# Two more chunks inverted in blocks of 32 steps, and the preparation dealt anew, in a chunked RWKV-7 and squared-ReLU kernel

## The chip, the cores and the metric

The kernel runs on one core of a Trainium2 chip, in float32. The metric is the device time of one execution in microseconds. A program of one core has one time; the times below are the median of a few runs, and one further execution was taken with the hardware profiler.

## What is computed

For each of 4 batches and 8 heads a state of 40 x 40 runs over 768 steps, and each step is read out before it changes the state. The result, 3072 tokens of 320 numbers, goes through a feed-forward layer with a squared ReLU.

```python
state = np.zeros((B, H, D, D))                     # B, H, S, D = 4, 8, 768, 40
for t in range(S):
    kt, vt, rt = k[:, :, t], v[:, :, t], r[:, :, t]
    wt, at, bt = w[:, :, t], a[:, :, t], b[:, :, t]
    y[:, :, t] = np.einsum('bhd,bhde->bhe', rt, state)
    Sa = np.einsum('bhde,bhe->bhd', state, at)
    state_decay = state * wt[:, :, None, :] - np.einsum('bhd,bhe->bhde', Sa, bt)
    state = state_decay + np.einsum('bhd,bhe->bhde', vt, kt)
...
x = y.transpose(0, 2, 1, 3).reshape(3072, 320)
h = np.maximum(x @ w_in, 0.0)                      # 320 x 2048
out = h * h @ w_out                                # 2048 x 320
```

## The kernel before

**Chunks and slots.** The 768 steps of a batch are cut into 6 chunks of 128 steps. There are 24 chunks, numbered so that the batch runs fastest: chunks 0 to 3 are the first chunks of the four batches, 4 to 7 the second ones. The main loop has one slot a chunk. A slot runs the chunk's `chain`: it brings in what the state gives, solves for the removed part x with the matrices T and N, updates the state, and makes the chunk's tokens (line 684, the last step of the chain). Within the same slot, in an order that is written out by hand (`woven` for slots 0 to 3, `sorted_slot` from slot 4 on), lie the preparation of the next chunk (`turn_rv`, `turn_k`, `make_a`, `make_rv`, `scale_kb`, `decay_state`), the feed-forward layer of chunks that are done (`second`), and the early part of chunks further ahead.

**Early parts.** `early` needs only w, a and b of a chunk. It takes cumulated products of w (lines 352 and 353), their reciprocals (357, 358), products with a and b (364, 365) and the triangular matrix `N` of the chunk, 128 x 128 for each head (line 372 ff.). It stores the decays (`kept_e`), the upper right block of N (`kept_n`), and what has to be inverted. The table `ahead` says which early parts a slot makes. A slot with two makes the first (`one`) at the places of the single one and the second (`two`) at later places; the stores of a second part leave after the slot's chain, together with the token moves and the loads of the next slot.

**The inversion on GpSimd.** Each head's chunk has two triangular blocks of 64 x 64 whose inverses the chain needs. GpSimd finds them by substitution (`solving`): for every step one product (line 448) and one subtraction (line 450), on 128 partitions, over all chunks of a *unit*. A unit is a run of chunks that are inverted together: chunk 0; 1; 2 and 3; 4 and 5; 6 and 7; 8 and 9; 10 to 13; 14 to 17; 18 to 21; 22 and 23 (units 0 to 9). `take` (line 420) loads a unit's blocks from `kept_q` or `kept_d` in device memory into `half_n`, and line 453 stores the inverses from `half_t` to `kept_t`. GpSimd's instructions run in their order, so a unit starts when the one before it is stored and when the blocks of all its chunks have landed. The main loop emits a unit when the early parts of all its chunks are done.

**Fine and coarse units.** The number `FINE` divides the units. Units below it are *fine*: their blocks are halved once more to 32 x 32 (31 steps instead of 63), stored in `kept_q`, with the block that joins two halves in `kept_m`. What the joining takes is done later by other engines in `inverses`: a transposition of the loaded inverses on VectorE (line 482), two activations (line 484), two times 16 products of 32 x 32 on TensorE, and copies (lines 494 and 501). A coarse unit's inverse comes from `kept_t` straight into T (line 464). Before, units 0 to 3 are fine.

**A unit in two pieces.** Unit 4, `AHEAD`, is emitted in two pieces: 33 steps after its load; then, when unit 5 can be emitted, the first 2048 words a row of unit 5 are loaded, the rest of unit 4 runs, and the rest of unit 5 is loaded.

**Loads.** All loads and stores but GpSimd's go through SyncE's queue, in the order in which they are written. `loads(j)` loads chunk j's decays (`dec`), k and b; r and v come one at a time through `fetch_next`. At the end of slot 3 the loads for slot 4's preparation of chunk 5 are issued as dec, k, b and then v. `later` holds a store back for a step or two; what stands behind it in that list waits with it.

Of the kernel before, what the change touches and what calls it, by code (L numbers as in the profile page):

```python
# [17 lines left out]
def kernel(  # L18
# [29 lines left out]
    HC = C // 2  # L48
# [11 lines left out]
    at = 0  # L60
# [31 lines left out]
    def new(name, shape, bufs):  # L92
        return work.tile(shape, FP32, tag=name, name=name, bufs=bufs)
# [7 lines left out]
    def tick():  # L101
        for entry in line:
            entry[0] -= 1
        while line and line[0][0] <= 0:
            line.pop(0)[1]()
# [10 lines left out]
    class Ring:  # L116
# [6 lines left out]
        def next(self):  # L123
            self.at = (self.at + 1) % len(self.tiles)
            return self.tiles[self.at]
# [10 lines left out]
    order = [(bb, c) for c in range(NCH) for bb in range(B)]  # L136
    loaded, early_loaded = {}, {}

    def fetch(ring, src, i):
        bb, c = order[i]  # L140
        t_ = rings[ring].next()
        nc.sync.dma_start(out=t_[:, :, :D], in_=src[bb, :, c * C:(c + 1) * C, :].rearrange("h t d -> t h d"))
        return t_
# [137 lines left out]
    def as_they_are():  # L281
# [4 lines left out]
        for f in range(NF):  # L286
# [8 lines left out]
    Q = HC // 2  # L295
# [2 lines left out]
    sizes = [1, 1] + [2] * 4 + [4] * ((len(order) - 12) // 4) + [2]  # L298
    units = [(sum(sizes[:u]), n) for u, n in enumerate(sizes)]

    FINE = 4
    SMALL = units[FINE][0]
    kept_q = dram.tile([SMALL, H, 2, 2, Q, Q], FP32, tag="q", name="kept_q")
    kept_m = [dram.tile([2, Q, H, Q], FP32, tag=f"m{i}", name=f"kept_m{i}") for i in range(SMALL)]
# [3 lines left out]

    classes = lambda u: 128 // (units[u][1] * (4 if u < FINE else 2) * H)
    kept_t = [dram.tile([classes(u), nb, H, 2, 2, Q // classes(u), Q] if u < FINE else [classes(u), nb, H, 2, HC // classes(u), HC], FP32,  # L310
                        tag=f"t{u}", name=f"kept_t{u}") for u, (_, nb) in enumerate(units)]
# [93 lines left out]

    part_of = lambda u: given[:, u % 3 * Q * Q:(u % 3 + 1) * Q * Q] if u < FINE else given


    EARLIER = Q * HC

    def take(u, queues, words=slice(None)):
        first, nb = units[u]
        if u < FINE:
            kept = kept_q[first:first + nb].rearrange("b h f k s t -> (b h f k) (s t)")
        else:
            kept = kept_d[u].rearrange("b h f w -> (b h f) w")
        cols = classes(u)
        rows = 128 // cols
        for col in range(cols):
            queues[col % len(queues)].dma_start(out=part_of(u)[col * rows:(col + 1) * rows, words], in_=kept[:, words])  # L420

    def solve(u, between={}):
        run(solving(u, between))

    def solving(u, between={}, stop=None):

        first, nb = units[u]
        fine = u < FINE
        size = Q if fine else HC
        cols = classes(u)  # L430
        rows = 128 // cols
        part = part_of(u)
        words = size // cols * size
        at = u * Q * Q // 2 if fine else 0
        ts = solved[:, at:at + words]
        nc.gpsimd.memset(ts, 0.0)
        for col in range(cols):
            nc.gpsimd.memset(ts[col * rows:(col + 1) * rows, col::size + cols], -1.0)
        t3 = ts.rearrange("p (j t) -> p j t", t=size)
        for s in range(size - 1):  # L440
            if s in between:
                between[s]()
            if s == stop:
                yield
            n, m_ = s // cols + 1, size - 1 - s
            at = s * size + s + 1 if s < Q else Q * HC + (s - Q) * (Q + 1) + 1
            p_ = new("half_p", [128, 528], 1)[:, :n * m_].rearrange("p (j t) -> p j t", j=n)
            nc.gpsimd.tensor_tensor(p_, part[:, at:at + m_].unsqueeze(1).to_broadcast([128, n, m_]),  # L448
                                    t3[:, :n, s:s + 1].to_broadcast([128, n, m_]), Alu.mult)
            nc.gpsimd.tensor_tensor(t3[:, :n, s + 1:], t3[:, :n, s + 1:], p_, Alu.subtract)  # L450
        to = kept_t[u]
        to = to.rearrange("n b h f k j t -> (n b h f k) (j t)") if fine else to.rearrange("n b h f j t -> (n b h f) (j t)")
        nc.gpsimd.dma_start(out=to, in_=ts)
# [331 lines left out]
    def run(gen):  # L785
        for _ in gen:
            tick()
# [28 lines left out]
    own = [nc.gpsimd]  # L816

    def flush():
        while line:
            tick()  # L820
# [58 lines left out]


    TOTAL = 12
    ahead = {0: (4, 5), 1: (6, 7), 2: (8, 9), 3: (10,), 4: (11,), 5: (12, 13)}
    ahead.update({i: (i + 8,) for i in range(6, 9)})
    ahead[9] = (17, 18)
    ahead.update({i: (i + 9,) for i in range(10, len(order) - 9)})

    pieces_in = {0: (4, TOTAL), 1: (6, TOTAL), 2: (6, TOTAL), 3: (7, TOTAL)}
    done = set(range(B))
    unit = unit_of[B]

    AHEAD, under_way = (FINE,), []

    def woven(i, g, ch):
        jobs = [(ch, 11, 0, TOTAL)]
        made = ahead.get(i, ())
        for j, m_ in enumerate(made):
            jobs.append((prepare(m_), 5, j * 5, TOTAL - 5 * (len(made) - 1 - j)))
        if i:
            ready[i + 1] = {}
            load(i + 1, ready[i + 1])  # L900
        jobs.append((rest(i + 1, ready[i + 1]), 9, 2, TOTAL))
        m_, end = pieces_in[i]
        jobs.append((some(rounded, 2 * m_), 2 * m_, 0, end))
        weave(*jobs)

    def fetch_next(i, *names):
        if i < len(order):
            loaded.setdefault(i, {}).update({nm: fetch(nm, {"k": k, "b": b, "r": r, "v": v}[nm], i) for nm in names})

    def loads(j):  # L910
        if j < len(order):
            n = ready.setdefault(j, {})
            n["dec"] = kept_here[j % 2]
            nc.sync.dma_start(out=n["dec"][:USED], in_=kept_e[j])
            fetch_next(j, "k", "b")
# [65 lines left out]
    for i in range(len(order)):  # L981
        tc.no_sync_barrier()
        g = ready.pop(i)
        ch = first_slot if i == 0 else g["chain"]
        done.update(ahead.get(i, ()))
        if i < B:
            woven(i, g, ch)
            n = ready[i + 1]
            n["chain"] = chain(i + 1, n)
            next(n["chain"])  # L990
            if i == B - 1:
                loads(i + 2)
                fetch_next(i + 2, "v")
        else:
            sorted_slot(i, g, ch)
        while unit < len(units) and all(m_ in done for m_ in range(len(order)) if unit_of[m_] == unit):
            flush()
            if under_way:

                take(unit, own, slice(0, EARLIER))  # L1000
                run(under_way.pop())
                take(unit, own, slice(EARLIER, Q * (HC + Q)))
            else:
                take(unit, own)
            if unit in AHEAD:
                under_way.append(solving(unit, stop=Q + 1))
                next(under_way[0])
            else:
                solve(unit)
            unit += 1  # L1010
    flush()
    second.rest()
# [30 lines left out]
```

## Time and profile before

| | |
|---|---|
| median of 3 runs | 1040.03 us (1037.89 to 1045.76) |
| the profiled execution | 1038.23 us |
| its span from first to last instruction | 1036.5 us |
| TensorE busy in the span | 907.5 us (88%) |
| its weight loads | 756.3 us (73%) |
| GpSimd busy | 672.7 us (65%) |
| VectorE busy | 484.4 us (47%) |
| ScalarE busy | 285.2 us (28%) |

The page gives busy time by engine and, below that, the span in 40 slices of 25.9 us, with a digit for the tenths in which the engine was busy (9 is 90% or more). PE is TensorE, PEld its weight load, DVE VectorE, ACT ScalarE, POOL GpSimd, SPq the queue of SyncE, which issues transfers. PEclk is the clock that TensorE was granted, in tenths of full speed, and DMA the mean busy share of the 16 DMA engines.

A row of a timeline has the start in us, the duration in us, engine, line and operation, what is written and read, how many such instructions stand together, and in brackets the idle time of the engine before them and what ended it. A row of the busy time by stage has the stretch, its length, the busy time of TensorE, its weight loads, VectorE, ScalarE and GpSimd with the number of instructions, then clock, DMA share and GB/s.

### The profile page before, as it was taken

How to read it: one execution, taken by the hardware profiler on the slowest of the kernel's cores; microseconds unless marked ns; L12 is line 12 of the kernel's file. 1: busy time of each engine (PE TensorE's matmuls, PEld its weight loads, DVE VectorE, ACT ScalarE, POOL GpSimd, SP SyncE). 2: the span in 40 equal slices, each digit the busy share in tenths (PEclk: the TensorE clock that was granted, in tenths of full speed). 3: DMA queues.
4: the chain of work that ended last, by engine and by line, in shares of the span. 5: the costliest groups of instructions: out<-in, count | busy, mean ns of one | idle time of the engine just before them, and what ended most of it. 6: DMA issues, size and time to landing. Idle time of an engine off the chain costs nothing.

```text
span 1036.5 us, 19696 instructions
## 1 busy us (share of the span) xinstructions
PE 907.5 (88%) x7728; PEld 756.3 (73%) x7728; DVE 484.4 (47%) x864; ACT 285.2 (28%) x663; POOL 672.7 (65%) x1128
## 2 busy tenths in 40 slices
PE   6465664684799999999599999999999999999998
PEld 5454563674688888888388888788888888887776
DVE  5556675765457346656066544624433233321111
ACT  3132423143323322332123222322222322232111
POOL 4788462898798359999599994999967981000000
PEclk9666565656799999999699999999999999999999
DMA  8977979795433894663785776553346434130000
GB/s 105 160 140 146 177 157 172 164 178 120 78 84 80 157 175 87 117 90 65 178 145 88 103 114 158 106 82 59 69 109 104 67 56 95 31 65 8 14 13 13
DMA packets 261376, 106.92 MB, mean 103 GB/s; under 512 B 244100, under 2 KB 250372, under 8 KB 259620
## 3 DMA queue, kind: packets, MB, share of 16 engines
q1 hardware_dynamic: 256756, 86.65, 47.5%
q0 software_dynamic: 3440, 18.88, 7.8%
q8 instruction: 61, 1.00, 0.4%
q10 hardware_dynamic: 1088, 0.13, 0.1%
q14 instruction: 31, 0.25, 0.1%
HBM read 72.47 MB, written 31.19 MB: 100 GB/s over the span
## 4 chain that ended last, share of the span: by engine, by line
PE 57%; POOL 14%; DMA 11%; DVE 5%; ACT 4%; issue 4%; SPq 4%; ACTq 0%; POOLq 0%; DVEq 0%
PE ps_f L87 30%; PE ps_c L87 12%; PE ps_w L87 9%; POOL half_t L450 7%; POOL half_p L448 6%; PE ps_w L316 3%; SPq L108 2%; DMA in_v<-in_v_dram 2%; DMA blocks<-kept_t 2%; DMA dec<-kept_e 1%; DMA half_n<-kept_d 1%; DMA kept_t<-half_t 1%; PE ps_c L651 1%; PE ps_c L560 1%; DMA in_k<-in_k_dram 1%
## 5 line engine op out<-in xcount | busy, mean ns | idle before, releaser
L448 POOL TENSOR_TENSOR half_p<-half_n,half_t 128x70 f32<-128x70 f32 (+52 forms) x502 | 298.3, 594 | 94.2 <-DMA half_n<-kept_d 43.5
L450 POOL TENSOR_TENSOR half_t<-half_t,half_p 128x70 f32<-128x70 f32 (+52 forms) x502 | 324.9, 647 | 39.3
L87 PE MATMUL ps_f<-w_out,hid 128*128 128x320 f32 x768 | 219.3, 435 | 0.0
L87 PEld LDWEIGHTS ps_f<-w_out,hid 128*128 128x128 f32 x768 | 141.3, 190 | 54.4 <-issue 3.4
L87 PE MATMUL ps_f<-tokens,w_in 128*128 128x256 f32 x672 | 158.7, 390 | 0.0
L87 PEld LDWEIGHTS ps_f<-tokens,w_in 128*128 128x128 f32 x672 | 127.5, 195 | 18.4 <-issue 1.0
L743 DVE TENSOR_TENSOR hid<-hid 128x512 f32<-128x512 f32 x96 | 88.8, 961 | 49.7 <-ACT hid L736 49.7
L736 ACT ACTIVATE hid<-ps_f 128x512 f32<-128x512 f32 x84 | 50.2, 598 | 97.9 <-PE ps_f L87 97.3
L684 DVE TENSOR_TENSOR tokens<-ps_c,dec 128x512 f32<-128x512 f32 x24 | 16.6, 691 | 92.2 <-PE ps_c L87 92.2
L532 DVE TENSOR_TENSOR f<-end,dec 128x4 f32<-128x4 f32 x20 | 7.1, 355 | 112.1 <-DMA dec<-kept_e 112.1
L352 DVE TENSOR_TENSOR_SCAN decay<-ps_w,ones 128x64 f32<-128x64 f32 x88 | 23.7, 270 | 65.7 <-PE ps_w L316 65.7
L87 PEld LDWEIGHTS ps_c<-xr,T 64*64 64x64 f32 x768 | 29.8, 148 | 32.9 <-issue 27.8
L615 ACT COPY xnT<-ps_c 64x512 f32<-64x512 f32 x24 | 13.9, 579 | 143.8 <-PE ps_c L87 143.7
L87 PE MATMUL ps_w<-decay,bT 40*128 40x128 f32 x352 | 31.9, 327 | 23.2 <-DVE decay L365 21.3
L372 ACT COPY N<-ps_w 128x512 f32<-128x512 f32 x24 | 14.1, 586 | 135.3 <-PE ps_w L87 106.6
L332 DVE TENSOR_TENSOR RV<-ps_w,upper 128x512 f32<-128x512 f32 x48 | 30.9, 686 | 42.4 <-PE ps_w L87 41.9
L87 PE MATMUL ps_f<-tokens,w_third 64*128 64x256 f32 x336 | 47.0, 391 | 3.9 <-DVE w_out L266 3.9
L510 DVE TENSOR_TENSOR kvT<-ps_w,dec 128x512 f32<-128x512 f32 x24 | 16.3, 681 | 70.7 <-ACT minus_x L638 33.6
L87 PE MATMUL ps_c<-xr,T 64*64 64x40 f32 x768 | 35.7, 242 | 15.2 <-DMA tokens<-tokens 12.8
L87 PEld LDWEIGHTS ps_w<-decay,bT 40*128 40x128 f32 x352 | 29.2, 231 | 26.7 <-issue 14.7
L332 DVE TENSOR_TENSOR RX<-ps_w,upper 128x512 f32<-128x512 f32 x48 | 30.9, 686 | 26.9 <-PE ps_w L87 26.8
L357 DVE RECIPROCAL decay<-decay 128x256 f32<-128x256 f32 x22 | 38.2, 1737 | 0.0
(136 smaller groups left out, 1484.0 us busy)
## 6 DMA issues: line engine op xcount, KB each, us to landing
kept_e<-decay SPq DMA_DIRECT2D x22, 633.8 KB
dec<-kept_e SPq DMA_DIRECT2D x22, 633.8 KB
hid<-in_moe_w_out_dram SPq DMA_DIRECT2D x16, 320.0 KB
half_n<-kept_d POOLq DMA_DIRECT2D x6, 768.0 KB, 11.9
in_w<-in_w_dram SPq DMA_DIRECT2D x24, 160.0 KB
in_ab<-in_b_dram SPq DMA_DIRECT2D x24, 160.0 KB
in_ab<-in_a_dram SPq DMA_DIRECT2D x24, 160.0 KB
in_k<-in_k_dram SPq DMA_DIRECT2D x24, 160.0 KB
```

Source lines behind the costliest of these rows:

```text
L87: nc.tensor.matmul(o, l_, r_, start=start, stop=True, skip_group_check=True)
L108: later(lambda: queue.dma_start(out=out_, in_=in_), steps)
L316: nc.tensor.transpose(p_[:, q * 128:(q + 1) * 128], pair(x_, q), ident)
L332: nc.vector.tensor_tensor(t_, p_, over4(upper), Alu.mult)
L352: nc.vector.tensor_tensor_scan(up[:, q, MID + 1:C + 1], wT[:, q, MID:], ones, 1.0, Alu.mult, Alu.mult)
L357: nc.vector.reciprocal(down[:, :, MID + 1:C + 1], up[:, :, MID + 1:C + 1])
L448: nc.gpsimd.tensor_tensor(p_, part[:, at:at + m_].unsqueeze(1).to_broadcast([128, n, m_]), t3[:, :n, s:s + 1].to_broadcast([128, n, m_]), ...
L450: nc.gpsimd.tensor_tensor(t3[:, :n, s + 1:], t3[:, :n, s + 1:], p_, Alu.subtract)
L510: nc.vector.tensor_tensor(kT, kT_, down[:, :, 1:C + 1], Alu.mult)
L684: nc.vector.tensor_tensor(t_, y_, g["up"][:, :, :C], Alu.mult)
L736: nc.scalar.activation(h_, p_.rearrange("p f t -> p (f t)"), Act.Relu)
L743: nc.vector.tensor_tensor(h_, h_, h_, Alu.mult)
```

## The change

Unit 4 (chunks 6 and 7) becomes fine. Its place in `half_t` is that of unit 0. Every unit is now emitted whole. In `ahead`, slot 4 makes chunks 11 and 12 and slot 5 makes 13 and 14, and from slot 6 to slot 14 slot i makes chunk i + 9; before, slot 4 made 11, slot 5 made 12 and 13, slots 6 to 8 made chunk i + 8, and slot 9 made 17 and 18. At the end of slot 3, v of chunk 5 is loaded ahead of dec, k and b.

```diff
-    FINE = 4
+    FINE = 5
...
-        at = u * Q * Q // 2 if fine else 0
+        at = u % 4 * Q * Q // 2 if fine else 0
...
-    ahead = {0: (4, 5), 1: (6, 7), 2: (8, 9), 3: (10,), 4: (11,), 5: (12, 13)}
-    ahead.update({i: (i + 8,) for i in range(6, 9)})
-    ahead[9] = (17, 18)
-    ahead.update({i: (i + 9,) for i in range(10, len(order) - 9)})
+    ahead = {0: (4, 5), 1: (6, 7), 2: (8, 9), 3: (10,), 4: (11, 12), 5: (13, 14)}
+    ahead.update({i: (i + 9,) for i in range(6, len(order) - 9)})
...
-    AHEAD, under_way = (FINE,), []
...
             if i == B - 1:
+                fetch_next(i + 2, "v")
                 loads(i + 2)
-                fetch_next(i + 2, "v")
...
-            if under_way:
-
-                take(unit, own, slice(0, EARLIER))
-                run(under_way.pop())
-                take(unit, own, slice(EARLIER, Q * (HC + Q)))
-            else:
-                take(unit, own)
-            if unit in AHEAD:
-                under_way.append(solving(unit, stop=Q + 1))
-                next(under_way[0])
-            else:
-                solve(unit)
+            take(unit, own)
+            solve(unit)
             unit += 1
```

## The prediction

> **What bounds the kernel now.** I read the forty slices first, then busy time by stage, the gaps on TensorE, GpSimd's own list and SyncE's queue. Slot i is the stretch that ends when line 684 writes chunk i's tokens: slots 1 to 5 end at 147.34, 201.93, 240.15, 304.21 and 341.63 us, slots 8 to 10 at 446.01, 482.61 and 538.25.
>
> ```profile
> PE   6465664684799999999599999999999999999998
> ...
> POOL 4788462898798359999599994999967981000000
> PEclk9666565656799999999699999999999999999999
> DMA  8977979795433894663785776553346434130000
> ```
>
> From the twelfth slice on TensorE is full, but for one slice. Before that, in slots 1 to 4, it is half busy while the DMA engines are near full. The same by slot (busy us of TensorE, weight loads, VectorE, ScalarE, GpSimd; clock; DMA):
>
> ```profile
> 377.29:411.65 34.36, 34.36 (x317) 29.28 (x314) 18.47 (x32) 10.10 (x24) 31.61 (x36) 1.00 0.64 106
> 446.01:482.61 36.60, 36.28 (x328) 30.99 (x326) 25.70 (x43) 10.12 (x24) 33.93 (x35) 1.00 0.58 91
> 482.61:538.25 55.64, 41.56 (x332) 34.50 (x330) 18.15 (x31) 11.70 (x28) 41.56 (x65) 0.82 0.67 138
> 641.35:678.05 36.70, 35.18 (x316) 29.77 (x314) 17.71 (x31) 10.11 (x24) 29.18 (x41) 1.00 0.62 116
> ```
>
> A slot with one early part is 34.36 us, all TensorE. Slot 10 is 55.64. TensorE's list says where it stood, and the chain of waits what ended it: GpSimd's store of unit 6 and the load of T.
>
> ```profile
> 509.01 1.08 PE L87 MATMUL ps_c<-xr,T 64*64 64x40 f32 x16 [12.82 <-DMA tokens<-tokens]
> ```
> ```profile
> 494.61 5.30 DMA kept_t<-half_t
> 500.61 8.31 DMA T<-kept_t
> ```
>
> GpSimd needed 134.9 us from the load of unit 6 (359.75) to its store (494.61). It began late not for want of time: it had stored unit 5 at 345.34 and waited for the blocks of chunk 13.
>
> ```profile
> 345.34 0.60 POOL L453 DMA_DIRECT2D kept_t<-half_t  x1 [0.30 <-POOL half_t L450]
> 359.75 1.03 POOL L420 DMA_DIRECT2D half_n<-kept_d  x2 [13.81 <-DMA kept_d<-N]
> ```
>
> SyncE's queue shows why. Slot 5's first early part (chunk 12) leaves at 334.71, its second (13) only at 351.64, behind the token moves and chunk 7's loads:
>
> ```profile
> 334.71 1.82 SPq L108 DMA_DIRECT2D kept_d<-N  x4
> ...
> 351.64 6.25 SPq L108 DMA_DIRECT2D kept_d<-N  x4
> ```
>
> Three further gaps on TensorE stand in slots 2 and 4, all on loads:
>
> ```profile
> 170.52 1.11 PE L316 MATMUL ps_w<-ident,in_k 128*128 128x128 f32 x4 [5.93 <-DMA in_k<-in_k_dram]
> ...
> 182.40 1.09 PE L316 MATMUL ps_w<-ident,in_w 128*128 128x128 f32 x4 [7.89 <-DMA in_w<-in_w_dram]
> ...
> 260.47 1.09 PE L316 MATMUL ps_w<-ident,in_v 128*128 128x128 f32 x4 [12.84 <-DMA in_v<-in_v_dram]
> ```
>
> **What the Trainium skill says.** "DMA: Bandwidth & Descriptors", section "Issuing engines are not separate DMA queues": transfers started by SyncE and GpSimd run on the same 16 engines and interleave. The trace agrees: from 161 to 183 us SyncE's queue takes 73.9% and GpSimd's 35.6% of the engines, more than 100% together, while slot 2's loads are late. "TensorE: Matmul & The Clock Gate", Part 1: after a few us of idling TensorE runs at half clock. Agreed: 0.50 granted between 500 and 513 us, and 16 rows of xr,T take 1.08 us against 0.66 us elsewhere, so a gap costs a little more than itself. "GPSIMD Engine Reference", section 8: GpSimd shares its SBUF interfaces with VectorE. Agreed: a line-450 subtraction of 273 elements took 1.13 us once and 0.71 us another time; units 4 and 5, the same 126 operations, took 76.7 and 80.9 us.
>
> **The change part by part**, against the profiled execution's 1038.23 us (span 1036.5 plus 1.7 around it), which lies 1.8 below the median and within the runs.
>
> *Unit 4 in blocks of 32.* Its compute becomes unit 3's, 27.1 us (121.25 to 148.38), for 76.7. Taken from 161.5, it ends near 201. Unit 5 then waits for chunk 9, loads near 211 in one piece, starts near 228 and ends near 309. GpSimd's 50 us are not on the path as such: unit 6 waits for chunk 13 in either case. Worth 0; if that cover were gone, unit 6 would be late by whatever unit 5 lacks of about 32 us of spare time.
>
> *Its transfers, slot 2.* The load at 161.5 falls from four of 384 KB to two of 256 KB, 1.05 MB less; the 1.57 MB took 35.6% of 22 us, 7.8 us of all engines, so 5.2 us come free beside the two late loads. Against it stand two extra kept_m stores for each of chunks 6 and 7, ahead of chunk 3's in_k in SyncE's queue: such issues took 0.56 to 1.71 us in slot 0, some 0.8 each, 3.2 us. I take -2, from -5 to +3.
>
> *Unit 5's load, slot 3.* It was split: 1 MB at 219.2, 0.5 MB at 257.8. Now 1.5 MB leave as soon as chunk 9's blocks have landed, about 211, and in_k, dec, r, v and b leave at 210.7 to 213.6. That is slot 2's picture: there dec was issued at 161.53 and read at 177.75, 16.2 us later. In slot 3 dec leaves at 211.13 and line 510 read it at 220.60 without a wait. 16.2 us would make that 227.3, 6.7 late, with TensorE's dec,kvT behind it. Bounds: nothing, or both waits of slot 2, 13.8. I take +6.
>
> *v of chunk 5 first, slot 4.* v left fourth, at 252.73, and landed at 260.34, 9.4 us after dec had left. Now it takes dec's place at 250.95, and GpSimd's store and load at 257 have gone. Landing 3.5 us after issue (my estimate; in_w took 5.04 at 177.22 on full engines), it comes at 254.5. dec, k and b go back by one issue, 4.05 us at most; line 532 reads dec at 269.9, with room. I take -6, from -3 to -7.
>
> *Early parts dealt anew.* Chunk 12 moves from slot 5 to slot 4, 13 becomes slot 5's first part, and so on to 18, alone in slot 9. A second part costs 36.60 - 34.36 = 2.24 us in its slot and 1.85 us in the next (to line 615: 8.16 us for 6.31): 4.1. Slot 4 gains it, slots 9 and 10 lose it: 0. Its VectorE work (two reciprocals of 1.7 us, eight scans of 0.18, two products of 0.6) fits a 9.7 us wait of VectorE in slot 4. If slot 4's waits hide it: -4; if not and VectorE is late: +2.
>
> *Joins of chunks 6 and 7.* 32x32 products cost TensorE 0.69 us twice a chunk; the two slots are full, so 1.4 each in slots 5 and 6, +2.8. The transposition (0.43), two activations (0.5 each) and eight copies (0.36) lie on engines that are busy 10 to 26 us of 36. If TensorE waits for the copies as once in slot 3 (1.60): +6.
>
> *Unit 6 begins earlier.* Chunk 13's blocks now leave where chunk 12's did, through 336.53; 1.9 us later (as 357.89 to 359.75) and 3.5 us for what slots 2 to 5 add (-2, +6, -6, +4.1, +1.4), the load starts at 341.9. 134.9 us on, the store is at 476.8, landed 5.3 later at 482.1. Slot 9 ends at 482.61 + 3.5 + 1.4 + 1 - 2.24 = 486.3, and T is asked for then (in slot 14 at 641.46, with slot 13's end at 641.35). TensorE reads T 11.6 us into a slot (13.5 from 341.63 to 355.13, less 1.85), at 497.9. Even with the 8.31 us that T took, it is there. Slot 10's surplus is 55.64 - 34.36 - 1.85 = 19.4. What is late next: unit 7's load now falls on the end of slot 9 as unit 8's did on that of slot 13, and slot 14 was 36.70 long, 2.3 over. So -17.1, from -19.4 to -10. Slot 14 keeps its 2.3, since unit 8's load and the slot move together: 0, or -2.3.
>
> *Unit 6's load, slot 6.* It now runs from 342 to 354, beside the token moves and dec at 350; before, VectorE got dec at 356.04 and then had 2.7 us to spare. +1, from 0 to +4.
>
> Sum: -2 + 6 - 6 + 0 + 2.8 - 17.1 + 1 = -15.3, 1038.2 - 15.3 = 1023.
>
> **The rivals.**
> *The collisions cost what slot 2 paid.* The loads of units 5, 6 and 7 all start with a slot's own dec. Should each hold up TensorE by 13.8 us (5.9 + 7.9) as unit 4's did in slot 2, that is 41.4 for the 9.3 that I have charged: 1055, slower. For it: DMA is full in slots 2 to 4. Against: unit 6's load at 359.75 met a full DMA (0.90) in slot 6 and TensorE stood for nothing. It decides for slower from 36.7 us together, 12.2 each.
> *The collisions hide and slot 10 is whole:* 9.3 less, and the second part in slot 4 hidden: 1010. For it: slots 6 to 9.
> *T is late again.* From the store's landing (482.1) and T's 8.3 us there are 7.5 us left to its use at 497.9; with unit 6 a further 15 us late TensorE stands 7.5 us: 1031. For it: chunk 13's place hangs on how slot 4 gets on with two parts.
> *The joins stall.* If blocks come late, VectorE stands (17.4 us in two waits in the first slots); 8.7 in each of slots 5 and 6 gives 1040, no change.
>
> **How the numbers follow.** My case 0.60 (1016 to 1030 from its bounds), hidden collisions 0.15, T late 0.12, joins 0.06, collisions 0.07. About 1% is what a measurement of this kernel can tell from no change: 1029.6 to 1050.4. Faster takes 0.58 of my case, 0.15 and 0.05 of late T; slower 0.07 and a hundredth. The range 1010 to 1036 leaves out the collisions, the joins, and the ends of the others.
>
> **What would show it.** Unit 6's load near 342 and its store near 477; slot 10 near 37 us; no wait for in_v over 8 us in slot 4; slot 3 some 6 us longer, with VectorE waiting for dec at line 510; slots 5 and 6 longer by 1.4. I am wrong if unit 6 starts after 350, if slot 3 or 6 grows by over 10 us, or if the wait for T is still there.

## The result and the profile after

The changed kernel takes 1029.16 us (median of 4 runs, 1028.86 to 1031.83) where the kernel before took 1041.12 beside it (median of 4 runs, 1037.89 to 1045.76); the ratio is 0.9887, with a 95% interval from 0.9845 to 0.9930. It is faster by 1.1%. The forecast was 1023. The profiled executions are 1028.86 and 1038.23 us, so 9.4 us were gained where the sum said 15.3.

The lines of the page of the changed kernel that answer to those shown of before:

```profile
PE   6364676667899969999999999999999999999998
...
POOL 4788463538860499995999977999958860000000
PEclk8667555656799969999999999999999999999999
DMA  8977978694465856279665685544354443130000
```

The gap of the twentieth slice has gone, but one that was not there before stands in the fifteenth, with the clock down to 0.6. GpSimd is idle ahead of it, in the thirteenth. By stage (slot 6, then slot 10):

```profile
340.43:392.71 52.28, 43.48 (x396) 37.08 (x394) 18.70 (x32) 13.83 (x34) 38.79 (x51) 0.84 0.64 115
...
496.63:530.99 34.36, 34.36 (x316) 29.29 (x314) 17.90 (x31) 10.11 (x24) 31.85 (x33) 1.00 0.65 108
```

Slot 10 is whole: 34.36 us for 55.64. Slot 6 has become the long one: 52.28 us for 35.66. Slot lengths in us, from one write of the tokens to the next, in all profiled executions (the runs are told below; slots 0 and 23, and those that are the same to 0.1 us everywhere, are left out):

```
slot                       1     2     3     4     5     6     7     9    10    14
before                 57.18 54.59 38.22 64.06 37.42 35.66 34.36 36.60 55.64 36.70
changed                58.02 49.87 44.65 59.41 39.16 52.28 35.19 34.37 34.36 34.37
early blocks           57.25 50.13 42.86 58.85 39.16 44.12 35.19 34.36 34.37 34.37
unit 6 held            56.87 49.93 45.11 59.06 40.81 51.19 35.19 34.37 42.84 34.36
early blocks, 6 held   56.85 49.16 44.28 59.34 39.15 36.91 35.19 34.37 51.36 42.04
unit 5 held            55.77 49.79 38.42 58.52 40.82 47.94 35.19 34.37 34.37 34.36
v last                 55.66 49.95 43.89 65.72 39.15 52.53 35.19 34.37 34.36 34.37
old deal               56.22 49.51 43.71 57.87 38.06 50.30 35.19 36.60 45.09 34.37
coarse unit 4          58.86 54.59 37.90 64.35 38.51 38.66 34.37 34.36 47.92 42.25
three edits            56.96 49.94 38.51 60.09 39.15 38.36 35.19 34.36 34.68 35.46
```

Part of the differences is not the work of an edit: slot 1, which the edits to later slots leave alone, is 55.66 to 58.02 us in the kernels that share it.

From before to changed, slots 0 and 1 together end where they did (147.34 us in both). Slot 2 gains 4.7 us, 3 loses 6.4, 4 gains 4.7, 5 loses 1.7, 6 loses 16.6, 7 loses 0.8, 9 gains 2.2, 10 gains 21.3, 14 gains 2.3: 9.6 us.

GpSimd's list shows the mechanism of slot 10 at work. It stands 34 us with unit 5 stored until chunk 13's blocks have landed, and stores unit 6 at 471.43 for 494.61 before:

```profile
302.17 0.60 POOL L453 DMA_DIRECT2D kept_t<-half_t  x1 [0.30 <-DMA kept_e<-decay]
337.20 1.03 POOL L420 DMA_DIRECT2D half_n<-kept_d  x2 [34.42 <-DMA kept_d<-N]
```

What happened in slot 6 is read from four lists. TensorE first, then the engine that it waited for, ScalarE:

```profile
372.49 1.12 PE L651 MATMUL ps_c<-ident,minus_x 128*128 128x128 f32 x4 [8.53 <-ACT minus_x L638]
```
```profile
369.95 0.91 ACT L484 ACTIVATE T<-blocks,which 128x256 f32<-128x256 f32 x2 [11.49 <-DMA blocks<-kept_t]
```

ScalarE stood 11.5 us at line 484, the first thing that chunk 7's join does there, until the transfer of `blocks` had landed. Behind it in ScalarE's order stand two ReLUs and the copy of minus_x that TensorE's next transposition reads. The blocks were late because their load was issued late (SyncE), 4.5 us before they landed, and dec, ahead of them in the same queue, was late too (VectorE):

```profile
344.05 10.58 SPq L108 DMA_DIRECT2D tokens<-tokens  x8
354.67 0.50 SPq L911 DMA_DIRECT2D dec<-kept_e  x1
...
365.47 1.39 SPq L470 DMA_DIRECT2D blocks<-kept_t  x2
```
```profile
360.64 0.17 DVE L532 TENSOR_TENSOR f<-end,dec 128x4 f32<-128x4 f32 x1 [9.18 <-DMA dec<-kept_e]
```

The eight token moves took 10.58 us to issue; for the first 6 of them GpSimd's 1.5 MB for unit 6 (issued at 337.20, first read at 350.09) were under way. After the wait TensorE ran at half clock:

```profile
372.40:385.80 13.40, 13.31 (x113) 12.62 (x113) 6.09 (x10) 1.45 (x5) 12.45 (x13) 0.51 0.18 50
```

The same instructions, from the transposition of minus_x to that of the state, took 6.5 us in slot 6 before (363.88 to 370.34) and 13.3 us here (372.49 to 385.76). The wait costs 8.5 us and the clock behind it 6.8: 15.3 of the slot's 16.6. The chain of waits of the changed kernel agrees: between 335 and 395 us it goes through SyncE's stores and loads to line 470, the transfer of blocks, line 484 and line 638 to TensorE.

### The profile page after: what moved, and what is told of

It reads as the page before. It is cut to its first block, busy times and chain, and to the rows that moved or that the text cites. A ratio compares the mean times of both kernels' runs of the same rounds, so it can differ in the third digit from the quotient of the medians.

```text
span 1027.2 us, 19900 instructions
## 1 busy us (share of the span) xinstructions
PE 907.8 (88%) x7856; PEld 756.9 (74%) x7856; DVE 482.8 (47%) x866; ACT 289.5 (28%) x675; POOL 624.2 (61%) x1056
## 4 chain that ended last, share of the span: by engine, by line
PE 74%; DMA 9%; DVE 4%; SPq 3%; ACT 3%; POOL 3%; issue 3%; DVEq 0%; ACTq 0%; POOLq 0%
PE ps_f L87 39%; PE ps_c L87 16%; PE ps_w L87 11%; PE ps_w L316 5%; DMA dec<-kept_e 2%; SPq L108 1%; DMA w_out<-in_moe_w_in_dram 1%; DMA in_k<-in_k_dram 1%; PE ps_c L651 1%; POOL half_t L450 1%; POOL half_p L448 1%; PE ps_c L560 1%; DMA blocks<-kept_t 1%; PE ps_c L622 1%; SPq L142 1%
## 5 line engine op out<-in xcount | busy, mean ns | idle before, releaser
L448 POOL TENSOR_TENSOR half_p<-half_n,half_t 128x70 f32<-128x70 f32 (+50 forms) x470 | 277.9, 591 | 93.2 <-DMA half_n<-kept_d 40.1
L450 POOL TENSOR_TENSOR half_t<-half_t,half_p 128x70 f32<-128x70 f32 (+50 forms) x470 | 300.5, 639 | 36.8
L87 PE MATMUL ps_f<-tokens,w_in 128*128 128x256 f32 x672 | 155.7, 385 | 0.0
L684 DVE TENSOR_TENSOR tokens<-ps_c,dec 128x512 f32<-128x512 f32 x24 | 16.6, 690 | 94.5 <-PE ps_c L87 94.5
```

What stands on the lines that cost most here:

```text
L87: nc.tensor.matmul(o, l_, r_, start=start, stop=True, skip_group_check=True)
L684: nc.vector.tensor_tensor(t_, y_, g["up"][:, :, :C], Alu.mult)
```

## The experiments

Where one time is given for an experiment, it is that of a single run.

**Chunk 7's blocks loaded in slot 5.** The first question was whether the join's late load or GpSimd's transfer beside it made slot 6 long.

```diff
-            blocks = new("blocks", [128, H, Q], 1)
+            blocks = new("blocks", [128, H, Q], 2)
...
         fetch_next(j + 1, "v")
+        if j + 1 == 7:
+            ahead_of = ready.setdefault(j + 1, {})
+            ahead_of["joining"] = inverses(j + 1, ahead_of)
+            next(ahead_of["joining"])
```

> The changed kernel with one edit: the loads that chunk 7's join needs (blocks, N, joins) are issued in slot 5, right behind v, instead of in slot 6 behind the token moves, dec, k, b and the stores of chunk 14; a second buffer for blocks lets them land early. Nothing is left out. Theory A (slot 6 grew because ScalarE stood 11.5 us at line 484 for chunk 7's blocks, with TensorE's transposition of minus_x behind it): the wait of TensorE for minus_x (8.5 us) and the half clock after it go, slot 6 falls from 52.3 to 37 to 39 us, about 1015 us in all. Theory B (slot 6 grew because GpSimd's load of unit 6, 1.5 MB at 337, held up the token moves and dec on the DMA engines): dec still comes at 360, slot 6 stays above 46 us, and the whole above 1022.

It took 1020.93 us (1019.13 to 1025.44), a ratio of 0.9825 to the kernel before (0.9782 to 0.9867). The wait for minus_x is gone, but slot 6 fell to 44.12 us only, between the two forecasts. What was left is a wait for dec on VectorE:

```profile
363.47 0.76 DVE L532 TENSOR_TENSOR f<-end,dec 128x4 f32<-128x4 f32 x1 [11.61 <-DMA dec<-kept_e]
```

So theory A holds for one part and theory B for another. TensorE stood 1.8 and 2.8 us in this slot and ran 3.4 us at half clock. Dec left later here, 18.2 us into the slot against 14.2 in the changed kernel: the early loads and unit 6's load now lie together ahead of it.

**Unit 6's load held until dec has landed.**

```diff
+            if unit == 6:
+                held = kept_here[1][:DP, UP, 0, :2]
+                nc.gpsimd.tensor_tensor(new("held", [DP, 2], 1), held, held, Alu.mult)
             take(unit, own)
```

> The changed kernel with one edit: before it loads unit 6, GpSimd reads two numbers a row of chunk 7's dec, so that the load of 1.5 MB starts only when dec has landed (about 356 instead of 337). Nothing is left out. Theory B (the load of unit 6 is what holds up slot 6): the token moves take 7 us again instead of 10.6, dec is there at 356 or before, slot 6 is 36 to 40 us; the load being some 19 us later, part of the wait for T returns in slot 10 (10 to 15 us). Theory A (the wait is for chunk 7's blocks, which stand behind all this in SyncE's queue): slot 6 stays at 47 to 56 us, because the blocks now travel beside the load instead; slot 10 pays little, since slot 6 was late as well, and the whole is 1029 to 1040.

It took 1037.52 us. The token moves were issued in 7.02 us again and dec was there at 355.41, as theory B says, yet slot 6 was 51.19 us: the blocks came no earlier. The load of unit 6, now issued at 356.20, lies ahead of them, and the loads of b and a before them took 3.81 and 5.20 us to issue (0.64 and 0.65 in the changed kernel).

```profile
355.41 0.17 DVE L532 TENSOR_TENSOR f<-end,dec 128x4 f32<-128x4 f32 x1 [2.67 <-DMA dec<-kept_e]
370.96 0.45 DVE L482 STREAM_TRANSPOSE spares<-blocks 128x256 f32<-128x256 f32 x1 [8.80 <-DMA blocks<-kept_t]
```

Slot 10 was 42.84 us, but TensorE did not stand for T in it: unit 6 was stored at 489.06, and slot 6 had held the slots back as well. What came late was dec. GpSimd's load of unit 7 left at 489.67, 7.1 us before slot 9 ended; T's two loads then took SyncE 5.46 us to issue (1.31 in the changed kernel), and dec, behind them, was waited for 9.6 us:

```profile
516.23 0.30 DVE L532 TENSOR_TENSOR f<-end,dec 128x4 f32<-128x4 f32 x1 [9.59 <-DMA dec<-kept_e]
```

TensorE then had only short waits behind VectorE, the longest of 1.23 us, but 10 us at half clock after them.

**Both.** The two edits together.

> The changed kernel with two edits: chunk 7's join loads in slot 5, and unit 6's load held until dec of chunk 7 has landed. Nothing is left out. Each alone left slot 6 long (44.1 and 51.2 us). If the join's loads and unit 6's load are the two causes and there is no third, slot 6 is 36.5 to 38.5 us. The 19 us by which unit 6 is late come back in slot 10, which then grows to 54 to 60 us, for slot 6 no longer hides them; about 1030 us in all. If a third cause is at work in slot 6, it stays above 41 us.

Slot 6 is 36.91 us, 1.25 above the kernel before, which leaves no room for a third cause beside the join's own work. Over this floor, 14.3 us are left with unit 6 held (51.19), 7.2 with early blocks (44.12), and 15.4 with neither (52.28): the two causes overlap, and either edit by itself hides the worth of the other. These are not the pure prices of the two, for each edit also moved what the other load meets, and the half clock behind a wait is in them, which differs by up to 4 us from run to run (see the next experiment). Slot 10 was 51.36, with TensorE standing for T. Slot 14 became 42.04, some 8 us over, which the expectation had not seen: unit 7 was now late as well, unit 8's load left 8.4 us before slot 13 ended, and dec was late in slot 14 as it was in slot 10 of the run before (VectorE waited 9.46 us). The total was 1036.59 us.

```profile
504.17 1.08 PE L87 MATMUL ps_c<-xr,T 64*64 64x40 f32 x16 [12.21 <-DMA T<-kept_t]
```

**Unit 5's load held until dec of chunk 4 has landed.** The same for slot 3's loss: `take(5)` and `solve(5)` are emitted in slot 3, behind the issue of chunk 4's dec.

```diff
             load(i + 1, ready[i + 1])
+        if i == 3:
+            held = kept_here[0][:DP, UP, 0, :2]
+            nc.gpsimd.tensor_tensor(new("held", [DP, 2], 1), held, held, Alu.mult)
+            take(5, own)
+            solve(5)
```

> The changed kernel with one edit: before it loads unit 5, GpSimd reads two numbers a row of chunk 4's dec, so that the 1.5 MB start when dec has landed in slot 3. Nothing is left out. If slot 3 grew by 6.4 us because this load held up dec (the prediction's step), slot 3 falls from 44.65 to 38 to 40 us, and line 510 waits for dec no longer. Unit 5 is 8 to 12 us later, which its 34 us of spare time before unit 6 cover: slots 5 to 10 keep their lengths within 1 us, unless slot 4 pays for transfers that now fall into it. If slot 3 grew for another reason, it stays above 43.

Slot 3 fell from 44.65 to 38.42 us and line 510 waits for dec no longer. In the changed kernel it stood as follows:

```profile
222.13 0.69 DVE L510 TENSOR_TENSOR kvT<-ps_w,dec 128x512 f32<-128x512 f32 x1 [8.02 <-DMA dec<-kept_e]
```

GpSimd loaded unit 5 at 213.27 for 206.61, and slot 4 paid nothing. It took 1019.23 us, but not all of this is the edit's. Slot 6 came out 4.3 us shorter than in the changed kernel although the waits in it are nearly the same:

```profile
365.42 1.11 PE L651 MATMUL ps_c<-ident,minus_x 128*128 128x128 f32 x4 [8.89 <-ACT minus_x L638]
```

The difference is the clock behind the wait. TensorE worked 4 us at half clock here and 13.4 in the changed kernel; the instructions from minus_x to the state took 9.1 us for 13.3. Slot 5 is 1.7 us longer, with 3.4 us at half clock in it.

**v last again.**

```diff
             if i == B - 1:
-                fetch_next(i + 2, "v")
                 loads(i + 2)
+                fetch_next(i + 2, "v")
```

> The changed kernel with one part undone: v of chunk 5 is issued behind dec, k and b again. The prediction's step says that the order is worth 6 us (between 3 and 7): slot 4 grows from 59.4 to 63 to 66 us and TensorE's wait for v from 4.3 to about 10. If it was GpSimd's transfers at 257, gone in the changed kernel in any case, that made v late, slot 4 stays within 1.5 us of 59.4.

It took 1033.22 us. Slot 4 is 65.72 us for 59.41, 6.3 more, and TensorE's wait for v 10.64 us for 4.28. In the changed kernel and in this run:

```profile
256.44 1.09 PE L316 MATMUL ps_w<-ident,in_v 128*128 128x128 f32 x4 [4.28 <-DMA in_v<-in_v_dram]
```
```profile
260.40 1.08 PE L316 MATMUL ps_w<-ident,in_v 128*128 128x128 f32 x4 [10.64 <-DMA in_v<-in_v_dram]
```

In the other runs with v first and unit 4 in blocks of 32, slot 4 is 57.87 to 60.09. The order of the loads does it.

**The early parts dealt as before.**

```diff
-    ahead = {0: (4, 5), 1: (6, 7), 2: (8, 9), 3: (10,), 4: (11, 12), 5: (13, 14)}
-    ahead.update({i: (i + 9,) for i in range(6, len(order) - 9)})
+    ahead = {0: (4, 5), 1: (6, 7), 2: (8, 9), 3: (10,), 4: (11,), 5: (12, 13)}
+    ahead.update({i: (i + 8,) for i in range(6, 9)})
+    ahead[9] = (17, 18)
+    ahead.update({i: (i + 9,) for i in range(10, len(order) - 9)})
```

> The changed kernel with one part undone: the early parts are dealt as in the kernel before (12 and 13 in slot 5, 17 and 18 in slot 9). Unit 4 is in blocks of 32 and every unit whole. The prediction's step says that unit 6 begins early because chunk 13 became a first part, not because GpSimd has less to do: unit 6's load then goes back to 350 to 360 us although GpSimd is free from about 300, and slot 10 stands for T again, 8 to 14 us with slot 6 as long as in the changed kernel (47 to 56 us). Slot 4 is 2 to 4 us shorter than 59.4, slot 9 is 36.6. About 1035 us. If less work on GpSimd were what counts, the load would stay near 337 and slot 10 at 34.4.

It took 1036.06 us. GpSimd was free at 301.30 and stood 51.66 us:

```profile
301.30 0.60 POOL L453 DMA_DIRECT2D kept_t<-half_t  x1 [0.30 <-POOL half_t L450]
353.56 1.03 POOL L420 DMA_DIRECT2D half_n<-kept_d  x2 [51.66 <-DMA kept_d<-N]
```

Less work on GpSimd starts nothing earlier without the new deal. Slot 10 is 45.09 us, as long as expected but not for the reason expected: TensorE did not stand for T, since slot 6 (50.30 us) had held the slots back too. Unit 7's load left at 488.24, 3.2 us before slot 9 ended, and slot 10's own loads were late beside it; TensorE stood 2.03 us for w and 2.88 behind VectorE, which had waited for dec:

```profile
517.51 0.65 DVE L532 TENSOR_TENSOR f<-end,dec 128x4 f32<-128x4 f32 x1 [13.44 <-DMA dec<-kept_e]
```

Slot 4 is 57.87 us and slot 5 38.06, so the second part in slot 4 costs about 1.5 us there and 1.1 in slot 5.

**Unit 4 in blocks of 64, in one piece.**

```diff
-    FINE = 5
+    FINE = 4
```

> The changed kernel with one part undone: unit 4 is inverted in blocks of 64 again, in one piece; the new deal and v first stay. No joins for chunks 6 and 7. GpSimd ends unit 4 near 256 and unit 5 near 350, so unit 6's load cannot leave at 337 but near 352, and T is late by 8 to 14 us in slot 10. Slot 2 is 54 to 55 us again, slot 3 38 to 39, slots 5 and 6 are 37 to 40 with no wait for blocks. If slot 6's 17 us in the changed kernel came from the join and from unit 6's load there, this kernel is as fast as the changed one or faster, 1022 to 1033 us; if the blocks of 32 are worth more than they cost, it is above 1036.

It took 1039.01 us: the blocks of 32 are worth more than they cost, even with slot 6 as it is. GpSimd got to unit 6 only when unit 5 was done, and in slot 10 (47.92 us) TensorE waited 8.52 us for T. In slot 14 (42.25 us) T was there; unit 8's load left 8.8 us before slot 13 ended, and VectorE waited 9.57 us for dec.

```profile
352.44 0.60 POOL L453 DMA_DIRECT2D kept_t<-half_t  x1 [0.30 <-POOL half_t L450]
353.14 1.03 POOL L420 DMA_DIRECT2D half_n<-kept_d  x2
```

Slot 2 is 54.59 us, as in the kernel before, so its gain in the changed kernel is unit 4's smaller transfers. Slot 4 is 64.35 us although v is first:

```profile
255.15 1.09 PE L316 MATMUL ps_w<-ident,in_v 128*128 128x128 f32 x4 [6.71 <-DMA in_v<-in_v_dram]
...
272.06 1.09 PE L316 MATMUL ps_w<-ident,in_w 128*128 128x128 f32 x4 [4.32 <-DMA in_w<-in_w_dram]
```

The wait for v ends before GpSimd's store and load (256.56 and 257.16) and lies among those of the other runs with v first (3.5 to 7.1 us). The wait for w, which none of them has, comes after, beside GpSimd's load. So the order shortens the wait for v here too, but with unit 4 in blocks of 64 slot 4 as a whole gained nothing (64.06 before, without a second part).

**Three edits together.** Early blocks, unit 5 held, and chunk 7's dec, k and b issued ahead of the token moves of slot 5:

```diff
-        step(on(ch))
+        step(on(ch), *[lambda: loads(j + 1)] * (i == 5))
         if more:
             later_chain = n["chain"] = chain(j, n)
             next(later_chain)
         run(ch)
-        loads(j + 1)
+        if i != 5:
+            loads(j + 1)
```

> The changed kernel with three edits, read slot by slot: chunk 7's join loads in slot 5 (as in the run with early blocks), unit 5's load held until dec of chunk 4 has landed (as in the run that holds unit 5), and, new, chunk 7's dec, k and b issued ahead of the token moves at the end of slot 5. Nothing is left out. With early blocks alone slot 6 was 44.1 us, and line 532 stood 11.6 us for dec, which left at 357 behind token moves slowed by unit 6's load. If that is the whole rest of slot 6's loss, dec now leaves some 7 us earlier and slot 6 is 37 to 40 us; slot 3 is 38 to 40 us as with the held load; about 1007 us in all. If the transfers are too many whatever their order, slot 6 stays at 42 to 46 us and the whole near 1013.

It took 1010.53 us (1007.24 to 1012.85), a ratio of 0.970 to the kernel before (0.9664 to 0.9736). Slot 6 is 38.36 us and slot 3 38.51. Dec came at 354.05, after 6.32 us of VectorE's waiting, and TensorE waited for none of it:

```profile
354.05 0.35 DVE L532 TENSOR_TENSOR f<-end,dec 128x4 f32<-128x4 f32 x1 [6.32 <-DMA dec<-kept_e]
```

This version beats both kernels, with unit 6's load where the changed kernel has it (3.2 us before the end of slot 5 in both). It has no stretch below full clock between 300 and 700 us.

## Why the prediction was right, and where it was off

The direction and the main gain were right; the forecast was 6 us too low, because one step was mis-sized by 14 us and several others, 9 us together, came out better than reckoned. That the total lies so near is partly luck, for these errors have opposite signs. One sign that I had named for being wrong did come, slot 6 longer by over 10 us.

- *Slot 10, unit 6 earlier* (-17.1 and -1.85 of the second part, together -18.95): -21.28 measured. The load left at 337.20 (forecast 341.9) and the store at 471.43 (476.8). That chunk 13's place in the deal decides when unit 6 starts, and not how busy GpSimd is, is shown by the run with the old deal; that the blocks of 32 must clear the way, by the run with unit 4 coarse; that a late unit 6 brings the wait for T back, by that run and by the one with both edits. The 2.3 us that I charged slot 10 for unit 7's load did not occur, nor did slot 14 keep its own 2.3. There was luck in this: unit 7's load left 24.6 us before the end of slot 9, where I had it 9 us before (477 and 486.3), because the long slot 6 held the slots back and not GpSimd. With slot 6 mended (three edits) it left 12.0 us before, and slots 10 and 14 were 34.68 and 35.46 us.
- *Unit 4's transfers* (slot 2, -2): -4.72. The wait for in_w fell from 7.9 to 3.4 us and that for in_k from 5.9 to 4.6; in_k was issued at 162.29 instead of 161.09, 1.2 us later, where I had charged 3.2 us for the two extra stores a chunk.
- *Unit 5's load* (slot 3, +6): +6.43, and holding the load took 6.23 of it back. Shown.
- *v first and the second part* (slot 4, -6 and +2.24): -4.65. v is worth 6.3 (shown), and the second part costs about 1.5 here.
- *Chunk 6's join and the rest of the second part* (slot 5, +1.4 and +1.85): +1.74. The second part is 1.1 of it (39.16 us against 38.06 with the old deal), the join 0.65 (against 38.51 with unit 4 coarse). The second part cost 2.6 us in all instead of 4.1.
- *Slot 6* (+1.4 for the join, +1 for unit 6's load): +16.62. This is the step that failed. I priced the join by the engines' busy time and by one wait of TensorE for its copies, and named the load of blocks only in the rival of the stalled joins, at 8.7 us a slot. What the runs show in its place: in this slot the load stands behind a second part's stores, the token moves and six loads; ScalarE's first join instruction holds back minus_x; and the clock behind the wait cost 6.8 us on top of 8.5, where I had a gap cost a little more than itself. The collision of unit 6's load with dec, bounded at 4 us, leaves 7.2 when the blocks are loaded early. The two together made 15.4.
- *Slot 7* (0): +0.83, the second half of chunk 7's products at its start (33 more instruction records than slot 8's 316), which I had put into slot 6.

Of the rivals, the collisions did come in slots 3 and 6 but not in slot 10, where the changed kernel escaped one that four of the runs show in slot 10 or 14; the stalled join came in one slot of the two. Neither was enough to turn the result.

## What to carry to other kernels

A step that is split among engines is priced by more than its work: its loads have a place in a queue, and the first instruction that reads them holds back everything behind it on an engine that runs in order. List for each moved step what stands ahead of its load in the issuing queue and what stands behind its first reader. When two waits overlap in one slot, removing either shows only part of its worth; run both, and both together. A large transfer from an engine with time to spare can be started a few microseconds later by letting it read what the urgent load brings: unit 5, with 34 us to spare, gave back 6.2 us in this way, while holding unit 6 by some 20 us, more than it had, made slot 10 17 us longer once slot 6 was short.

## What the runs showed that was not expected

After TensorE had stood for 8.5 us in slot 6, it worked without a gap at half clock for 13.4 us (0.51 granted) before it was back at full speed; in slot 10 before, after 12.8 us, the same took 11.9 us (0.55). The Trainium skill ("TensorE: Matmul & The Clock Gate", Part 1) gives some 3.4 us of work for the return. The runs show both: between 300 and 700 us of all ten profiled executions, eight waits of 7 to 13 us were followed by about 4 us of work at half clock twice (unit 5 held, old deal) and by 10 to 14 us six times. Read in steps of half a microsecond, the stretches below full clock, waits included, lasted 3.4, 10.2, 17.1 or 20.5 us, each close to a multiple of 3.4. Nor does it need a long wait: in slot 10 with unit 6 held, waits of 1.23 us and less, some 2 us together, came before 10.2 us at half clock. What decides the length is not shown. So one and the same wait in slot 6 cost 15.3 us in the changed kernel (8.5 and 6.8) and 11.5 with unit 5 held (8.9 and 2.6), and the total of a single run does not tell an edit worth 4 us.

The length of slots 10 and 14 goes with how long before the slot's start GpSimd's load of the next unit leaves, for the slot's own dec is loaded soon after that start (in us):

```
run                   slot   load ahead of its start   length
changed                 10                       24.6    34.36
old deal                14                       14.5    34.37
three edits             14                       13.4    35.46
three edits             10                       12.0    34.68
before                  14                       11.2    36.70
coarse unit 4           14                        8.8    42.25
early blocks, 6 held    14                        8.4    42.04
unit 6 held             10                        7.1    42.84
old deal                10                        3.2    45.09
```

TensorE stood for T in none of these. The last row carries the rest of a second part as well (1.85 us), and no run moved the load alone.

The issue of a transfer is itself slowed: eight token moves took SyncE 10.58 us beside GpSimd's load of 1.5 MB and 7.02 us with that load held back, so what stands behind them in the queue is late before its own transfer has begun. It need not be GpSimd's load: with three edits the same eight moves, now behind dec, k and b, took 10.78 us after that load had landed.
